# Per-head attention, wide fp32 loads for the first two batches and kept-back FFN units in a fused attention and SwiGLU kernel

## The chip, the cores and the metric

The kernel runs on one core of a Trainium2 chip. The metric is the device time of one execution in microseconds (us), taken as the median of several; lower is better. The kernel before takes 501.65 us (4 runs, 501.2 to 505.33). All times of this document come from runs of the state "fast", except where one is said to be otherwise. "Span" is the time from the first to the last instruction of the profiled execution; it lies about 2 us below the device time of the same run. The profiled run of the kernel before took 504.84 us.

Engines: PE is TensorE (matmuls; PEld is its weight load), ACT is ScalarE, DVE is VectorE, POOL is GpSimd, SP is SyncE. A line number such as L204 is a line of the kernel that the profile belongs to, so L204 of one kernel is not L204 of another.

## The reference

Block-causal attention (blocks of 64 in a sequence of 576, 8 batches, 8 heads of 64) feeds an RMS-normalised SwiGLU feed-forward network (FFN) over the 4608 tokens.

```python
def _attn_ref(q, k, v):                       # each (8, 8, 576, 64), float32
    scores = q @ k.transpose(0, 1, 3, 2) / np.sqrt(64)
    mask = (pos[:, None] // 64) >= (pos[None, :] // 64)
    scores = np.where(mask, scores, -1e9)
    attn = softmax(scores)                    # written out in the original
    return attn @ v

def _moe_ref(x, w_gate, w_val, w_out, rms_g): # x (4608, 512), d_ff = 1536
    xn = x / np.sqrt(np.mean(x * x, -1, keepdims=True) + 1e-6) * rms_g
    g = xn @ w_gate
    return (g / (1 + np.exp(-g)) * (xn @ w_val)) @ w_out
```

## The kernel before

The attention of one batch at a time is interleaved with the FFN of the 512-token chunk that earlier batches have completed. A chunk is 16 "units": 12 `ffn_up` units (8 matmuls of 512 columns each) and 4 `ffn_down` units (12 matmuls each). A list `units` holds them; attention code calls `run_unit()` between its stages, so that PE has FFN work while ACT computes exponentials. The order that the program text gives is a priority: a scheduler at build time places each instruction in its engine's own queue, and moves ready instructions up past ones that it believes will wait.

All loads that cast from fp32 to bf16 are issued by POOL. Q and K arrive as rows of 64 values, and a DMA transpose on the SP queue turns them.

```python
    def load_head(b, h, i):
        ...
        nc.gpsimd.dma_start(out=QKN[i][:, hp, kb:kb + NC, ds],
                            in_=k[b, h, BLK:S, :].rearrange("(c p) d -> p c d", p=P))
        nc.gpsimd.dma_start(out=QKN[i][:, hp, 1:NC + 1, ds], in_=q[...])
        nc.gpsimd.dma_start(out=VN[i][:, :, h, 0:D], in_=v[...])

    def transposes(b, hp):
        QKT = tp.tile([P, NBK, P], BF16, name="QKT")
        nc.sync.dma_start_transpose(out=QKT, in_=QKN[i][:, hp, :, :])
    ...
    def norm_stats(b):
        ...
        for t in range(NC + 1):                # ACT: sums of squares
            ...
            nc.scalar.activation(out=sq, in_=XN[:, t, :], func=AF.Square, accum_out=ss[:, t:t + 1])
        nc.gpsimd.tensor_scalar(out=rr, in0=ss, ...)                     # POOL
        nc.gpsimd.tensor_tensor(out=rs, in0=rr, in1=mhalf, op=ALU.pow)   # POOL
        ...
        for t in range(NC + 1):                # DVE
            nc.vector.tensor_scalar(out=XS[:, t, :], in0=XN[:, t, :], scalar1=rs[:, t:t + 1], ...)
    ...                                        # norm_transpose: PE transposes XS, ACT copies to XT
    for b in range(B):
        steps = load_batch_steps(b + 1, (b + 1) % 2) if b + 1 < B else []
        for hp in range(HP):
            ...
            for n, st in enumerate(attention_pair(b, hp)):
                st()
                run_unit()
            for _ in range(3):
                if steps:
                    steps.pop(0)()             # loads of the next batch
            ...
        norm_stats(b)
        run_unit()
        norm_transpose(b)
        while (chunks + 1) * TOKC <= (b + 1) * S:
            add_chunk(chunks)
            chunks += 1
```

What matters below is the end of each batch, called the boundary: the last values matmul on PE, normalisation `XN` on DVE, five squares on ACT, `rr` and `rs` on POOL, `XS` on DVE, transposes of `XS` on PE, `XT` on ACT, and only then the next chunk's FFN.

The softmax here doesn't subtract the row's maximum and nothing guards it: scores larger than these inputs give would overflow.

## Time and profile before

| what | read from | value |
|---|---|---|
| first score matmul | timeline of PE | 15.5 us |
| first FFN matmul | timeline of PE | 90.8 us |
| boundary to boundary (first transpose of `XS`), seven cycles | timeline of PE | 57.4, 49.5, 49.8, 49.0, 46.7, 46.5, 45.6 us |
| from the last boundary to the end | timeline of PE, span | 71.3 us |
| spacing of FFN matmuls | chain of work that ended last: 4 in 0.86 us | 0.216 us |

First some lines of the profile's page: the span, busy time by engine, and then the span in 40 equal slices, where each digit is the busy share in tenths (for PEclk the clock granted to PE, for DMA the mean share of the 16 DMA engines).

```profile
span 503.1 us, 7011 instructions
PE 387.4 (77%) x2534; PEld 205.0 (41%) x2576; DVE 215.5 (43%) x528; ACT 239.1 (48%) x481; POOL 204.4 (41%) x323
PE   0363005999149995999699879979997999699996
POOL 8995279898945533553365435130001000100000
PEclk9965655999759997999799989998999999799999
DMA  6999999999978887798789859461223201001102
```

The first seven slices (88 us) are thin on PE, while POOL and the DMA engines are busy. Then PE is mostly at 9 with gaps once per batch.

The timeline of PE around one boundary shows start, length in us, line, what was done and how many; in brackets, the idle time before it and what ended it.

```profile
184.39 0.41 PE L207 MATMUL Xb<-VN_92,PT 128*128 128x65 bf16 x8
184.64 2.75 PE L283 MATMUL fps<-WO,HT 128*128 128x512 bf16 x12
...
189.72 0.38 PE L163 MATMUL st<-QKT 128*128 128x512 bf16 x1 [1.87 <-ACT PT L166]
194.13 0.61 PE L253 MATMUL fps<-ident,XS 128*128 128x128 bf16 x4 [4.03 <-DVE XS L243]
```

From the last values matmul (184.8) to the first transpose of `XS` (194.1) pass 9.3 us; 1.87 + 4.03 us are idle. The timeline of POOL at the same boundary:

```profile
191.19 0.81 POOL L102 DMA_DIRECT2D QKN_94<-in_q_dram  x1
192.08 0.20 POOL L237 TENSOR_SCALAR rr<-ss 128x5 f32<-128x5 f32 x1
192.36 1.19 POOL L240 TENSOR_TENSOR rs<-rr,mhalf 128x5 f32<-128x5 f32 x1
```

The last square was ready on ACT at 189.2 us (its read-out starts at 189.00 and takes 0.19). POOL was issuing loads of the batch after next, which the scheduler had put ahead of `rr`, and reached `rr` at 192.08.

### The profile page before, as it was taken

The page shows a single profiled execution, that of the slowest core. Times are in us where ns is not written, and L with a number is a line of the kernel's source. Part 1 is how long each engine was busy: PE and PEld are TensorE (multiplying, and loading weights), DVE is VectorE, ACT ScalarE, POOL GpSimd, SP SyncE. Part 2 cuts the span into 40 slices and gives each one's busy share as a digit, 9 for nine tenths or more (in the row PEclk, how much of TensorE's full clock was granted, in tenths as well). Part 3 has the DMA queues.
Part 4 walks back from the last instruction along what each step waited for, and adds up shares of the span by engine and source line. Part 5 has one row for each costly group of instructions (what it writes and reads, how often), then busy time and mean ns, then how long its engine had stood idle before and what let it go on. Part 6 is the DMA issues. An engine that isn't in the chain of part 4 may idle for free.

```text
span 503.1 us, 7011 instructions
## 1 busy us (share of the span) xinstructions
PE 387.4 (77%) x2534; PEld 205.0 (41%) x2576; DVE 215.5 (43%) x528; ACT 239.1 (48%) x481; POOL 204.4 (41%) x323
## 2 busy tenths in 40 slices
PE   0363005999149995999699879979997999699996
PEld 0232003555035543554455445536554455344442
DVE  3111002682018711771286138616742772274570
ACT  1252204645336555555545655565656655432331
POOL 8995279898945533553365435130001000100000
PEclk9965655999759997999799989998999999799999
DMA  6999999999978887798789859461223201001102
GB/s 41 108 106 165 205 121 162 119 130 140 159 60 73 95 134 86 62 98 129 88 78 84 133 79 83 54 137 38 38 59 103 34 1 63 22 1 44 42 1 84
DMA packets 184627, 43.47 MB, mean 86 GB/s; under 512 B 174352, under 2 KB 179984, under 8 KB 184592
## 3 DMA queue, kind: packets, MB, share of 16 engines
q0 software_dynamic: 120512, 18.89, 51.3%
q1 hardware_dynamic: 64080, 24.13, 22.8%
q8 instruction: 20, 0.33, 0.3%
q14 instruction: 15, 0.12, 0.1%
HBM read 37.75 MB, written 9.44 MB: 94 GB/s over the span
## 4 chain that ended last, share of the span: by engine, by line
PE 48%; issue 21%; POOL 15%; DMA 13%; ACT 1%; DVE 0%; POOLq 0%; SPq 0%; ACTq 0%
PE fps L266 15%; PE fps L270 14%; PE fps L283 9%; PE st L163 5%; DMA QKT<-QKN_94 5%; DMA WO<-in_moe_w_out_dram 4%; POOL QKN_91 L100 2%; PE fps L253 2%; POOL QKN_91 L102 2%; DMA WV<-in_moe_w_val_dram 2%; PE Xb L207 2%; POOL VN_95 L104 2%; POOL VN_92 L104 2%; POOL rs L240 1%; DMA QKN_94<-in_k_dram 1%
## 5 line engine op out<-in xcount | busy, mean ns | idle before, releaser
L166 ACT ACTIVATE PT<-st 128x512 bf16<-128x512 f32 x192 | 108.6, 600 | 120.1 <-PE Xa L178 67.1
L163 PE MATMUL st<-QKT 128*128 128x512 bf16 (+3 forms) x286 | 72.2, 348 | 73.2 <-DMA QKT<-QKN_94 30.4
L266 PE MATMUL fps<-XT,WG 128*128 128x512 bf16 x416 | 113.2, 384 | 2.6 <-ACT XT L254 1.3
L270 PE MATMUL fps<-XT,WV 128*128 128x512 bf16 x417 | 111.4, 381 | 0.5
L273 ACT ACTIVATE th<-fps 128x512 f32<-128x512 f32 x108 | 64.2, 599 | 78.5 <-PE fps L266 67.1
L283 PE MATMUL fps<-WO,HT 128*128 128x512 bf16 x423 | 97.6, 379 | 0.5
L275 DVE SCALAR_TENSOR_TENSOR u<-th,fps 128x512 f32<-128x512 f32 x108 | 73.7, 686 | 49.6 <-ACT th L273 49.1
L277 DVE TENSOR_TENSOR HT<-u,fps 128x512 bf16<-128x512 f32 x108 | 73.4, 685 | 7.5 <-PE fps L266 0.5
L173 DVE MEMSET PT<- 64x64 uint32 x128 | 12.6, 112 | 140.9 <-ACT PT L166 138.2
L270 PEld LDWEIGHTS <-WV 128*128 128x128 bf16 x432 | 42.5, 98 | 52.0 <-issue 2.5
L163 PEld LDWEIGHTS <-QKT 128*128 128x128 bf16 x288 | 28.3, 109 | 81.8 <-DMA QKT<-QKN_94 30.8
L283 PEld LDWEIGHTS <-HT 128*128 128x128 bf16 x432 | 41.5, 98 | 45.8
L266 PEld LDWEIGHTS <-WG 128*128 128x128 bf16 x432 | 40.7, 99 | 38.5 <-issue 2.6
L207 PEld LDWEIGHTS <-PT 128*128 128x128 bf16 x800 | 41.7, 103 | 21.1 <-ACT PT L179 4.0
L253 PE MATMUL fps<-ident,XS 128*128 128x128 bf16 x160 | 20.3, 283 | 32.7 <-DVE XS L243 32.7
L286 ACT ACTIVATE ob<-fps 128x512 f32<-128x512 f32 x36 | 21.4, 593 | 49.5 <-PE fps L283 49.5
L243 DVE TENSOR_SCALAR XS<-XN,rs 128x512 bf16<-128x512 f32 x40 | 16.5, 481 | 57.9 <-POOL rs L240 57.9
L237 POOL TENSOR_SCALAR rr<-ss 128x5 f32<-128x5 f32 x8 | 1.6, 196 | 91.3 <-ACT sq L234 90.9
L253 PEld LDWEIGHTS <-XS 128*128 128x128 bf16 x160 | 15.4, 130 | 51.5 <-DVE XS L243 49.1
L104 POOL DMA_DIRECT2D VN_95<-in_v_dram x32 | 25.2, 800 | 23.8 <-PE Xb L207 21.4
L104 POOL DMA_DIRECT2D VN_92<-in_v_dram x32 | 25.8, 814 | 19.8 <-PE Xb L207 17.5
L100 POOL DMA_DIRECT2D QKN_94<-in_k_dram x32 | 25.6, 800 | 19.7 <-DMA QKT<-QKN_94 16.1
(51 smaller groups left out, 337.7 us busy)
## 6 DMA issues: line engine op xcount, KB each, us to landing
out_dram<-ob SPq DMA_DIRECT2D x36, 256.0 KB, 2.0
QKN_91<-in_k_dram POOLq DMA_DIRECT2D x32, 64.0 KB, 3.1
QKN_91<-in_q_dram POOLq DMA_DIRECT2D x32, 64.0 KB, 3.2
VN_92<-in_v_dram POOLq DMA_DIRECT2D x32, 64.0 KB, 3.0
QKN_94<-in_k_dram POOLq DMA_DIRECT2D x32, 64.0 KB, 3.1
QKN_94<-in_q_dram POOLq DMA_DIRECT2D x32, 64.0 KB, 3.4
VN_95<-in_v_dram POOLq DMA_DIRECT2D x32, 64.0 KB, 3.4
WG<-in_moe_w_gate_dram POOLq DMA_DIRECT2D x4, 384.0 KB, 12.1
```

The source lines that it names most:

```text
L100: nc.gpsimd.dma_start(out=QKN[i][:, hp, kb:kb + NC, ds], in_=k[b, h, BLK:S, :].rearrange("(c p) d -> p c d", p=P))
L104: nc.gpsimd.dma_start(out=VN[i][:, :, h, 0:D], in_=v[b, h, BLK:S, :].rearrange("(c p) d -> p c d", p=P))
L163: nc.tensor.matmul(st[:, o:o + n], w, qt(lo, n), start=True, stop=True)
L166: nc.scalar.activation(out=PT[:, BLK + bank * TOKC:BLK + bank * TOKC + o], in_=st[:, 0:o], func=AF.Exp, scale=SM_SCALE)
L207: ins = nc.tensor.matmul(dst, w, r, start=(n == 0), stop=(n == len(mms) - 1))
L253: nc.tensor.transpose(xt[:, o:o + P], XS[:, t, p * P:(p + 1) * P], ident)
L266: nc.tensor.matmul(pg, WG[:, p, m * P:(m + 1) * P], XT[:, p, t0:t0 + TOKC], start=(p == 0), stop=(p == HP - 1))
L270: nc.tensor.matmul(pv, WV[:, p, m * P:(m + 1) * P], XT[:, p, t0:t0 + TOKC], start=(p == 0), stop=(p == HP - 1))
L273: nc.scalar.activation(out=th, in_=pg, func=AF.Tanh, scale=0.5)
L275: nc.vector.scalar_tensor_tensor(out=u, in0=th, scalar=1.0, in1=pg, op0=ALU.add, op1=ALU.mult)
L277: nc.vector.tensor_tensor(out=HT[:, m, :], in0=u, in1=pv, op=ALU.mult)
L283: nc.tensor.matmul(po, HT[:, m, s * P:(s + 1) * P], WO[:, m, :], start=(m == 0), stop=(m == NMC - 1))
```

## The change

Intent: shorten the load stage by bringing Q and K of batches 0 and 1 in as fp32 in runs of 1536 bytes on the SP queue, with casts on DVE and ACT and PE transposes instead of DMA transposes; handle one head at a time instead of pairs, with unshifted chunks of 128 keys; and hold FFN units back, so that there is some left to run at the boundary. The core of the diff:

```diff
+    WIDE = 2
+    def load_wide(b, h0, h1):
+        hs = slice(h0, h1)
+        for dst, src in ((QW, q), (KW, k)):
+            nc.sync.dma_start(out=dst[:, hs, :, :].rearrange("p h s d -> p h (s d)"),
+                in_=src[b, hs, :, :].rearrange("h (p s) d -> p h (s d)", s=SLOT))
     ...
     def transposes(b, hp):
+        if b < WIDE:
+            QT, KA, KB = views
+            nc.gpsimd.memset(KA[D:P, :], 0.0)
+            nc.gpsimd.memset(KB[0:D, :], 0.0)
+            for src, n in ((QW, 0), (KW, 1)):
+                ...                              # cast to bf16 (DVE or ACT)
+                    nc.tensor.transpose(t[:, s * PQ:(s + 1) * PQ], ...)
+                ...                              # copies from PSUM to QKT
+        else:
+            nc.sync.dma_start_transpose(out=T, in_=QKN[b % 2][:, hp, :, :])
     ...
-    def run_unit():
-        if units:
+    def run_unit(keep=0):
+        if len(units) > keep:
             units.pop(0)()
     ...                                          # prologue: V of batch 0, weights, V of batch 1
+    LAG = 5
     for b in range(B):
+        for h in range(H):
             ...
+            st0()
+            run_unit(LAG - 2 if h else 0)
+            st1()
+            if pending is not None:
+                head_values(*pending)
+            pending = (b, h, state)
+            run_unit(LAG - 2)
+            ...                                  # three load steps of the next batch
+        head_values(*pending)
+        pending = None
+        run_unit()
         norm_stats(b)
         run_unit()
         norm_transpose(b)
```

## The prediction

> **What bounds the kernel now.** TensorE, but not everywhere. The table of windows shows three stages.
> (a) 0 to about 91 us: loads. TensorE is busy about 24 us of the first 87.5; the DMA share is 1.0 to 1.8. The timeline shows the first score matmul at 15.5 us, waits for the transposed Q/K inside batch 0 (up to 6.7 us), then 28.2 us before batch 1, whose loads stand in the POOL queue behind the weights. The first FFN matmul starts at 90.8 us.
> (b) 91 to 437 us: one batch of attention plus one 512-token FFN chunk per cycle. The first takes some 57 us, with another load wait (PE busy 7.6 of 25 us from 125 to 150); the next ones 49.5, 49.8, 49.2, 48.5, 46, 42. An FFN matmul starts every 0.216 us, so 144 of them are 31 us and, with scores (5.2), values (3.4) and transposes (1.1), from spacings in the timeline, about 41 us are needed. The excess of 5 to 8 us lies at the batch boundary: the queue of FFN units is empty there (17 slots for 16 units), and PE waits for squares, POOL's `rr`/`rs` (held 3 us behind descriptor issues), `XS`, `XT` (waits of 1.9 and 4.0 us).
> (c) 437 to 503 us: two pure FFN chunks, 66 us, at full PE rate.
>
> **What the change does.** Q and K of batches 0 and 1 come as fp32 in 1536-byte runs on the sync queue instead of 256-byte runs through POOL; 32 DMA issues of 0.8 us and the small tails leave POOL, and 8 of 32 DMA transposes (4.2 to 4.4 us each) vanish. Added per head pair: two casts (768 elements; estimate 0.8 us each, from 0.60 us for 512 on ACT), 12 PE transposes, three copies from PSUM (about 0.7 us each, from 0.74 us for the 576-wide `XT` copy), two POOL clears. Batch 0 becomes ACT-bound at an estimated 5.6 us per pair (eight exponentials plus cast and copy). The Trainium skill, "DMA: Bandwidth & Descriptors", section "Why small descriptors are slow (HBM only)", states a fixed overhead per packet; here 174352 of 184627 packets are under 512 B, and no run shows the overhead itself yet.
> Score columns (3136 to 3200 per pair) and value matmuls: neutral. Keeping units back gives two FFN units (3.5 to 5 us) at the boundary and one after it.
>
> **On the critical path.** Stage (a): all of it. If the POOL clears run early, FFN starts near 48 us; if they stand behind the weight issues, which block on earlier DMAs, near 75 us. I take 60, a gain of 31. Stage (b): the first cycle loses its load wait (about 14 us), the other boundaries shrink to about 2 us: seven cycles of about 43 us, 301 instead of 346, a gain of 45. Stage (c): unchanged, 66, plus 3 for odds and ends.
> Sum: 60 + 301 + 69 = 430 us, range 413 to 452. Faster by over 2%: 0.96; within 2%: 0.03; slower: 0.01.
>
> **What would show it.** Right: first FFN matmul at 48 to 75 us; no wait over 10 us of score matmuls for a DMA transpose after batch 1; boundary waits of the `XS` transposes under 3 us; cycles 42 to 44.5 us; FFN matmuls still 0.216 us apart; packets on the software queue about 18,000 fewer; mean granted clock above 0.902. Wrong: cycles still near 49 us, or PE waiting for QKT.
>
> **What would make it wrong.** POOL clears stuck behind weights; batch 2's loads, behind weights and batch 1's V, arriving late; the scheduler not placing kept units in the boundary; POOL's `rr` still waiting behind descriptor issues.

## The result, and the profile after

The changed kernel takes 479.34 us (4 runs, 478.51 to 480.27), 0.954 of the kernel before (95% interval 0.9492 to 0.9589). Ratios here and below are the mean time of one kernel's fast runs over that of the kernel before in the same rounds, so not quite the ratio of the medians. The direction was right; the time lies 49 us above the predicted 430 and outside the stated range.

| | before | predicted | after |
|---|---|---|---|
| first score matmul, us | 15.5 | | 39.5 |
| first FFN matmul, us | 90.8 | 60 | 80.2 |
| seven cycles, us | 344.5 | 301 | 328.2 |
| their mean, us | 49.2 | 43 | 46.9 |
| last boundary to the end of the span, us | 71.3 | | 73.0 |

The same lines of the page for the changed kernel:

```profile
span 476.7 us, 7703 instructions
PE 389.7 (82%) x2854; PEld 207.7 (44%) x2896; DVE 240.6 (50%) x553; ACT 265.7 (56%) x571; POOL 153.3 (32%) x212
PE   1206725999699969996999699979988997999996
POOL 6628799325442454245424540220000001000000
PEclk9999975999799989998999899999999999899999
DMA  9999999659975897689758962590433001001002
```

There is now an empty place at slice 3 (24 to 36 us), where PE does nothing. The waits of PE, longest first in total (us in total, times, longest us), name it:

```profile
PE fps L287 <- DVE XS L269: 29.4, 8, 9.7
PE st L204 <- POOL QKT L159: 21.0, 1, 21.0
```

One wait of 21.0 us is for L159, a POOL clear of half of a K tile. The clear itself is short. The timeline of POOL shows where it stands:

```profile
13.01 1.00 POOL L132 DMA_DIRECT2D WG<-in_moe_w_gate_dram  x1 [4.38 <-DMA VN_95<-in_v_dram]
15.24 0.74 POOL L134 DMA_DIRECT2D WV<-in_moe_w_val_dram  x1 [1.23 <-DMA VN_95<-in_v_dram]
...
28.82 0.82 POOL L138 DMA_DIRECT2D WO<-in_moe_w_out_dram  x1 [3.38 <-DMA WV<-in_moe_w_val_dram]
33.08 0.88 POOL L95 DMA_DIRECT2D VN_96<-in_v_dram  x1 [3.43 <-DMA WG<-in_moe_w_gate_dram]
35.94 0.69 POOL L87 DMA_DIRECT2D VN_96<-in_v_dram  x1 [1.98 <-DMA WV<-in_moe_w_val_dram]
37.92 0.82 POOL L138 DMA_DIRECT2D WO<-in_moe_w_out_dram  x1 [1.29 <-DMA WG<-in_moe_w_gate_dram]
38.78 0.63 POOL L159 MEMSET QKT<- 64x640 bf16 x1
```

Between 8.6 and 37.9 us POOL stands still for 18 us in seven waits (4.38, 1.23, 2.37, 3.38, 3.43, 1.98, 1.29), each for an earlier load to land, before it can issue the next weight or V load. The clear comes last in that queue, at 38.78 us; the first score matmul follows at 39.46 us. The Trainium skill, "DMA: Bandwidth & Descriptors", section "Anatomy of one DMA — SWDGE (gpsimd) path", says that DMA engines do not wait on semaphores and that such a wait happens on the issuing sequencer before dispatch. This trace agrees: the waits lie on POOL, and a clear that depends on none of those loads waited with them.

The steady boundary of the changed kernel, on PE and then on POOL:

```profile
211.23 0.47 PE L237 MATMUL X<-VN_96,PT_100 128*128 128x65 bf16 x10
211.54 4.26 PE L320 MATMUL fps<-WO,HT 128*128 128x512 bf16 x19
217.62 0.38 PE L204 MATMUL st<-QKT 128*128 128x320 bf16 x2 [1.31 <-ACT PT_97 L208]
221.09 0.40 PE L287 MATMUL fps<-ident,XS 128*128 128x128 bf16 x4 [3.10 <-DVE XS L269]
...
225.34 2.75 PE L320 MATMUL fps<-WO,HT 128*128 128x512 bf16 x11
```

```profile
217.42 0.75 POOL L106 DMA_DIRECT2D QKN_93<-in_q_dram  x1
218.24 0.20 POOL L263 TENSOR_SCALAR rr<-ss 128x5 f32<-128x5 f32 x1
218.50 0.79 POOL L104 DMA_DIRECT2D QKN_93<-in_k_dram  x1
219.31 1.20 POOL L266 TENSOR_TENSOR rs<-rr,mhalf 128x5 f32<-128x5 f32 x1
```

From the last values matmul (211.7) to the first transpose of `XS` (221.1) pass 9.4 us: the chain is as long as before. In it run 19 matmuls of kept units instead of 12, and a third kept unit (225.34) comes only after the transposes. So the boundary gained seven matmuls, about 1.5 us, and the cycle went from 49.4 us (mean of cycles two to four, before) to 47.8 us. POOL again reaches `rr` late: the last square was ready at 216.6 us, `rr` starts at 218.24, and one more load issue was put between `rr` and `rs`. After batch 0 it is worse: the last square is ready at 64.7 us and `rr` starts at 72.82 us:

```profile
72.82 0.20 POOL L263 TENSOR_SCALAR rr<-ss 128x5 f32<-128x5 f32 x1
```

### The profile page after: what moved, and what is told of

It is laid out like the page before. It is cut to its first block, busy times and chain, and to the rows that moved or that the text cites. A ratio compares the mean times of both kernels' runs of the same rounds, so it can differ in the third digit from the quotient of the medians.

```text
span 476.7 us, 7703 instructions
## 1 busy us (share of the span) xinstructions
PE 389.7 (82%) x2854; PEld 207.7 (44%) x2896; DVE 240.6 (50%) x553; ACT 265.7 (56%) x571; POOL 153.3 (32%) x212
## 3 DMA queue, kind: packets, MB, share of 16 engines
q0 software_dynamic: 100576, 16.53, 46.0%
## 4 chain that ended last, share of the span: by engine, by line
PE 43%; issue 27%; POOL 12%; DMA 11%; ACT 5%; DVE 1%; POOLq 0%; ACTq 0%; SPq 0%; DVEq 0%
PE fps L308 12%; PE fps L304 12%; PE fps L320 9%; PE st L204 4%; DMA WG<-in_moe_w_gate_dram 4%; PE fps L287 3%; DMA QKT<-QKN_93 3%; DMA VN_95<-in_v_dram 3%; PE X L237 2%; POOL rs L266 2%; DMA QKT<-QKN_94 2%; POOL QKN_93 L104 1%; POOL QKN_94 L104 1%; POOL QKN_93 L106 1%; POOL VN_95 L95 1%
## 5 line engine op out<-in xcount | busy, mean ns | idle before, releaser
L304 PE MATMUL fps<-XT,WG 128*128 128x512 bf16 x411 | 110.4, 383 | 1.1 <-ACT XT L290 0.2
L312 DVE SCALAR_TENSOR_TENSOR th<-th,fps 128x512 f32<-128x512 f32 x108 | 74.3, 688 | 51.0 <-ACT th L311 50.6
L204 PE MATMUL st<-QKT 128*128 128x512 bf16 (+4 forms) x320 | 70.2, 307 | 31.9 <-POOL QKT L159 21.0
L314 DVE TENSOR_TENSOR HT<-th,fps 128x512 bf16<-128x512 f32 x108 | 74.2, 687 | 11.4 <-PE X L237 0.9
L204 PEld LDWEIGHTS <-QKT 128*128 128x128 bf16 x384 | 36.7, 101 | 63.3 <-POOL QKT L159 21.3
L320 PEld LDWEIGHTS <-HT 128*128 128x128 bf16 x432 | 41.1, 98 | 45.6 <-issue 3.1
L208 ACT ACTIVATE PT_97<-st 128x512 bf16<-128x512 f32 x48 | 26.8, 595 | 35.8 <-PE st L204 32.4
L287 PE MATMUL fps<-ident,XS 128*128 128x128 bf16 x160 | 18.5, 266 | 29.4 <-DVE XS L269 29.4
L208 ACT ACTIVATE PT_98<-st 128x512 bf16<-128x512 f32 x48 | 27.7, 606 | 18.4 <-PE st L204 14.5
L290 ACT ACTIVATE XT<-fps,gscale 128x512 bf16<-128x512 bf16 (+7 forms) x64 | 25.9, 520 | 17.5 <-PE fps L287 17.5
L208 ACT ACTIVATE PT_99<-st 128x512 bf16<-128x512 f32 x48 | 27.4, 599 | 12.5 <-PE st L204 6.3
L249 DVE TENSOR_TENSOR XN<-X,rd 128x320 f32<-128x320 f32 x64 | 31.4, 491 | 2.0
L260 ACT ACTIVATE sq<-XN 128x512 bf16<-128x512 f32 x40 | 25.1, 627 | 11.6 <-DVE XN L249 10.9
L208 ACT ACTIVATE PT_100<-st 128x512 bf16<-128x512 f32 x48 | 27.0, 601 | 6.7 <-PE X L204 3.4
L104 POOL DMA_DIRECT2D QKN_93<-in_k_dram x24 | 18.4, 766 | 38.2 <-DMA QKT<-QKN_93 37.9
## 6 DMA issues: line engine op xcount, KB each, us to landing
WG<-in_moe_w_gate_dram POOLq DMA_DIRECT2D x4, 384.0 KB, 11.8
```

The lines of the kernel that those rows point to most:

```text
L104: nc.gpsimd.dma_start(out=t[:, hp, kb:kb + NC, ds], in_=k[b, h, 0:TAIL, :].rearrange("(c p) d -> p c d", p=P))
L204: nc.tensor.matmul(dst[:, o0:o0 + n], KT[:, k0:k0 + P], QT[:, lo:lo + n], start=True, stop=True)
L208: nc.scalar.activation(out=PT[:, o:o + o0], in_=dst[:, 0:o0], func=AF.Exp, scale=SM_SCALE)
L249: nc.vector.tensor_tensor(out=xn_tiles[b][:, :, h * D:(h + 1) * D], in0=xv[:, :, 0:D], in1=rd.to_broadcast([P, NQT, D]), op=ALU.mult)
L287: nc.tensor.transpose(x[:, t * P:(t + 1) * P], XS[:, t, p * P:(p + 1) * P], ident)
L290: nc.scalar.activation(out=xt_tiles[t][:, p, a - t * TOKC:e - t * TOKC], in_=x[:, a - b * S:e - b * S], func=AF.Copy, scale=gscale[:, p:p ...
```

## The experiments

Theory A: POOL's order costs the missing time. The clears of the wide path stand behind weight loads, and `rr`/`rs` behind load issues. Theory B (rival): the bytes of the first 90 us and the early start of the loads are the limit, so that reordering POOL gains nothing. A second pair of theories is about the part that did bring the gain: the kept units, the wide loads, or the per-head pipeline. All kernels below gave correct results.

| run | us, median | ratio to the kernel before | first FFN matmul, us | mean of seven cycles, us |
|---|---|---|---|---|
| after | 479.34 | 0.954 | 80.2 | 46.9 |
| a1_clear_dve | 465.03 | 0.9239 | 68.1 | 46.6 |
| a2_rs_first | 460.48 | 0.9131 | 72.1 | 45.5 |
| a3_both | 445.01 | 0.8818 | 56.3 | 45.5 |
| a4_nolag | 506.46 | 1.0051 | 80.4 | 51.3 |
| b1_wide0 | 478.54 (fast runs) | 0.954 | 83.5 | 47.2 |
| b2_before_lag | 487.22 | 0.9668 | 89.4 | 46.8 |
| b3_units | 429.01 | 0.8517 | 57.6 | 43.3 |
| b4_defer | 425.31 | 0.8444 | 50.6 | 44.0 |
| c1_wide0_fixed | 452.03 | 0.8969 | 82.8 | 42.9 |
| c2_before_fixed | 453.05 | 0.9003 | 89.8 | 42.2 |
| c3_units_no_rs | 459.83 | 0.9123 | 69.4 | 46.0 |

The kernel before had medians of 503.44 to 505.04 us in the rounds of the experiments. The times of first matmuls and cycles are those of the profiled execution. b1_wide0 had one slow run among its four, which is left out.

### a1_clear_dve: the clears leave POOL

```diff
-            nc.gpsimd.memset(KA[D:P, :], 0.0)
-            nc.gpsimd.memset(KB[0:D, :], 0.0)
+            nc.vector.memset(KA[D:P, :], 0.0)
+            nc.vector.memset(KB[0:D, :], 0.0)
```

> The two clears of QKT go from POOL to DVE, nothing else changes. Theory (POOL's order): the 21 us wait of score matmuls for the POOL clear goes, the first score matmul moves from 39.5 us to about 20 us and the first FFN matmul from 80 us to about 60 us; time about 460 us, less gain if the small statistic rr then stands behind load issues on POOL. Rival (the startup is bound by the bytes of the weights and of Q/K/V, so that the order on POOL does not matter): the first FFN matmul stays within 4 us of 80 us, time 475 us or more.

Measured: 465.03 us. The first score matmul moved from 39.5 to 12.9 us, more than expected, but the first FFN matmul only from 80.2 to 68.1 us. The caveat in the expectation is what happened: the last square of batch 0 was ready at 49.7 us, and `rr` started at 60.65 us, behind load issues that themselves waited for weights. B falls in its strong form (12 us were to be had), but this edit alone frees only half of them.

### a2_rs_first: loads issued behind rs

```diff
-        nc.gpsimd.tensor_tensor(out=rs, in0=rr, in1=mhalf, op=ALU.pow)
+        last_rs[0] = nc.gpsimd.tensor_tensor(out=rs, in0=rr, in1=mhalf, op=ALU.pow).ins
 ...
+    def load_step(steps):
+        with tc.issue_after(last_rs[0]):    # order in POOL's queue only, no wait
+            steps.pop(0)()
 ...
-                    steps.pop(0)()
+                    load_step(steps)
```

> The loads of batch b+1 are issued on POOL only behind rr and rs of batch b-1; the clears stay on POOL. Theory (rr/rs are held behind load issues): the wait of XS for rs shrinks by 8 us after batch 0 and by 2 to 3 us at each of the next four or five boundaries, first FFN matmul at about 72 us, time about 460 us. Rival (the loads need that head start, or the boundary is bound elsewhere): waits for QKT come up or the cycles stay at 47 to 48 us, time 470 us or more.

Measured: 460.48 us, first FFN matmul at 72.14 us as expected, cycles 46.7, 45.8, 44.7, 44.8, 44.8, 46.0, 46.0 us. `rr` now starts within 0.2 us of the last square at every boundary, as here on POOL:

```profile
202.80 0.20 POOL L264 TENSOR_SCALAR rr<-ss 128x5 f32<-128x5 f32 x1 [23.59 <-ACT sq L261]
```

From the last values matmul (197.8 us) to the first transpose of `XS` (204.85) pass 7.0 us instead of 9.4. The waits of PE for `XS` fell from 29.4 us in all to 18.4 us, and no wait of PE for a DMA transpose came up: the loads did not need their head start. B falls for the cycles. One detail of the expectation is wrong: after the first two boundaries the wait for `XS` itself fell by 0.7 us at most. Of the 3.4 us that the cycle from 173.00 to 221.09 lost (the one from 160.15 to 204.85 in a2_rs_first), 1.1 us are less busy time of PE, at a granted clock of 1.00 against 0.96, and 2.3 us less idle time, 1.6 us of it in waits of scores for exponentials.

### a3_both: both edits

> Both edits. Theory: the gains add, first FFN matmul at 50 to 55 us, cycles about 45.5 us, time 440 to 448 us. Rival (bytes bind once POOL's order is right): first FFN matmul at 65 us or later, or waits for QKT over 5 us, time 455 us or more.

Measured: 445.01 us; first FFN matmul 56.3 us. In a3_both POOL's queue reaches `rr` early and waits for ACT, the right way round (timeline of POOL in a3_both):

```profile
36.63 0.87 POOL L138 DMA_DIRECT2D WO<-in_moe_w_out_dram  x1 [3.91 <-DMA WG<-in_moe_w_gate_dram]
49.51 0.20 POOL L264 TENSOR_SCALAR rr<-ss 128x5 f32<-128x5 f32 x1 [12.01 <-ACT sq L261]
49.79 1.20 POOL L267 TENSOR_TENSOR rs<-rr,mhalf 128x5 f32<-128x5 f32 x1
```

The gains add, within the range given (the first FFN matmul came 1.3 us later than the range said). 80.2 − 56.3 = 24 us of the start were POOL's order.

### a4_nolag: no unit kept back

```diff
-    LAG = 5
+    LAG = 2
```

> LAG = 2 in the changed kernel: no FFN unit is kept back. Theory (the kept units fill the boundary): each boundary wait of the XS transposes grows from about 2.5 us to 6 us or more, time 495 to 505 us. Rival (the kept units do little, because the scheduler orders by its own model): within 5 us of 479 us.

Measured: 506.46 us, as slow as the kernel before (1.0051, 1.0001 to 1.0101). The first FFN matmul stays at 80.4 us, the cycles are 55.7, 51.7, 52.9, 51.6, 49.2, 49.9, 47.9 us. The table of windows gives, for a stretch, its length, then the busy time (and number of instructions) of PE, PEld, DVE, ACT and POOL, the granted clock, the DMA share and GB/s. The third full cycle of a4_nolag, and the same cycle in the changed kernel:

```profile
183.14:236.01 52.87, 45.88 (x332) 24.70 (x333) 25.59 (x62) 29.36 (x66) 20.04 (x27) 0.89 0.88 94
```

```profile
173.00:221.09 48.09, 43.21 (x327) 23.38 (x333) 25.86 (x62) 29.98 (x66) 20.10 (x28) 0.96 0.91 100
```

The theory's time is right, its detail is not: the waits for `XS` did not grow to 6 us (3.86 us at this boundary, 32.3 us in all against 29.4). Of the 4.8 us more per cycle, 2.7 us are more busy time of PE at a lower granted clock (0.89 against 0.96) and 2.1 us more idle time, much of it in short waits of scores for exponentials near the end of the batch (over the run 40 waits with 18.3 us in all, against 22 with 10.2 us). My reading is that with 18 slots for 16 units the finer pipeline uses its units up before the batch ends. Inside the changed kernel, the kept units are worth its whole gain.

### b1_wide0: the wide loads undone

```diff
-    WIDE = 2
+    WIDE = 0
 ...
-    load_wide(0, 0, 2)
-    ...
+    for hp in range(HP):
+        clear_qkn(0, hp)
+    load_qk_tail(0)
+    ...                     # Q, K, V of batch 0 by POOL, then the weights; batch 1 in the loop
```

> The changed kernel with the wide fp32 loads undone (WIDE = 0): Q and K of batches 0 and 1 come through POOL in 256-byte runs and DMA transposes as in the kernel before; per-head pipeline and kept units stay. Theory (the wide loads' gain was eaten by the clears waiting on POOL): first FFN matmul at about 90 us instead of 80 and a load wait before batch 1 as before; time 487 to 495 us. Rival (the wide loads carry the change): 500 us or more.

Measured: 478.54 us, the median of three fast runs (478.32, 478.54, 485.39; one more run, 486.53, was slow; with it the median is 481.97), ratio 0.954, interval 0.9455 to 0.9625. The trace is that of the run of 485.39 us, hardly faster than the slow one. Neither the theory's time (487 to 495 us) nor the rival's holds: the time is that of the change as delivered. Without the wide loads the score matmuls wait for DMA transposes (45.8 us in five waits, 16.2 the longest), and yet the first FFN matmul comes only 3.3 us later than with them. As delivered, no gain of the wide loads can be told from noise.

### b2_before_lag: kept units alone in the kernel before

```diff
-                st()
-                run_unit()
+                st()
+                run_unit(3 if hp or n else 0)
 ...
+        run_unit()
         norm_stats(b)
         run_unit()
```

> The kernel before with kept units alone: three FFN units held back during a batch, one more slot before the statistics. Theory (kept units fill the boundary in any pipeline): waits of the XS transposes and the empty slots shrink, cycles from 49 us to 46 to 47 us, time 483 to 491 us. Rival (they only make up for a loss that the finer per-head slots bring, as the run without them stood level with the kernel before): within 5 us of the kernel before.

Measured: 487.22 us, 0.9668; later cycles 47.4, 47.4, 46.2, 45.2, 43.9, 43.9 us. The theory holds for the time: a few lines bring 3.3 of the 4.6% that the whole change brought. The waits for `XS` after the first boundary shrank less than it says, from 17.2 to 14.9 us in all.

### b3_units: both POOL edits and two more kept units

```diff
-    LAG = 5
+    LAG = 7
 ...
         norm_stats(b)
+        run_unit()
+        run_unit()
         run_unit()
```

> Both POOL edits plus two more kept units run between the statistics and the transposes (LAG = 7). Theory (PE still idles 2 to 3 us at each boundary for want of work): the wait of the XS transposes goes from 18 us in all to under 5 us, cycles about 43 us, time 428 to 434 us. Rival (the boundary is no longer the limit): 440 us or more.

Measured: 429.01 us; cycles 42.2, then 43.4 to 43.7 us. The waits of PE for `XS` are 4.3 us in all, in 22 pieces. One boundary in b3_units on PE, and the cycle before it in the table of windows:

```profile
216.54 0.61 PE L237 MATMUL X<-VN,PT 128*128 128x65 bf16 x15
216.99 1.03 PE L309 MATMUL fps<-XT,WV 128*128 128x512 bf16 x4
217.85 7.93 PE L321 MATMUL fps<-WO,HT 128*128 128x512 bf16 x36
225.62 0.46 PE L288 MATMUL fps<-ident,XS 128*128 128x128 bf16 x2
```

```profile
182.19:225.62 43.43, 42.65 (x333) 22.47 (x332) 25.60 (x62) 29.91 (x66) 20.26 (x28) 1.00 1.05 111
```

The chain still takes 8.5 us (217.1 to 225.6); matmuls of kept units fill it without a gap, and the granted clock stays at 1.00. This is the boundary that I had predicted for the change.

### b4_defer: batch 1's first casts behind the end of batch 0

Built on b3_units. The casts of batch 1's first head pair are queued on DVE behind the last `XN` of batch 0 and on ACT behind its last square:

```diff
         norm_stats(b)
+        if nxt < WIDE:
+            with tc.issue_after(last_sq[0]), tc.issue_after(last_xn[0]):
+                transposes(nxt, 0)
 ...
```

> As b3_units, and the casts of batch 1's first head pair are queued on DVE and ACT behind the last normalisation and the last square of batch 0. Theory (in the run with both edits these casts wait in order for the load of batch 1 and hold up the end of batch 0): first FFN matmul from about 56 us to about 49 us, time about 7 us below b3_units. Rival: batch 1 then starts later by as much, same time as b3_units within 3 us.

Measured: 425.31 us, 3.7 us below b3_units. Between the two: the first FFN matmul came 7.0 us earlier (50.6 us), and the first cycle gave 5.0 us of it back (47.2 instead of 42.2 us). It is the fastest version, 0.8444 of the kernel before (0.8403 to 0.8486); its slowest run (425.98 us) is below the fastest of b3_units (428.39 us).

### c1_wide0_fixed: b3_units without the wide loads

> b3_units with the wide loads undone as in b1_wide0 (there is then no clear to move): rs ahead of the loads, LAG = 7. Theory (the wide loads are worth about 20 us once no clear waits behind the weights): first FFN matmul at 80 to 84 us against 57.6 us in b3_units, later cycles 43.5 us, time 448 to 456 us. Rival (the wide loads are worth nothing in any setting, as they were in the change as delivered): within 5 us of 429 us.

Measured: 452.03 us, 23 us above b3_units, with the first FFN matmul at 82.8 us against 57.6 us. So next to b3_units the wide loads, with their PE transposes, are worth 23 us; in the change as delivered they were worth nothing that could be measured. But the 23 us are not free of POOL's order. The loads of batch 1 are issued before any `rs` exists, so the edit cannot put them behind one: the last square of batch 0 is ready at 54.4 us, and `rr` starts 16.5 us later, behind these loads. From 49.8 to 65.5 us PE waits for Q and K of batch 1 (PE, then POOL):

```profile
65.53 1.03 PE L204 MATMUL st<-QKT 128*128 128x512 bf16 x3 [15.78 <-DMA QKT<-QKN]
70.88 0.20 POOL L264 TENSOR_SCALAR rr<-ss 128x5 f32<-128x5 f32 x1
```

FFN work of the first chunk could have filled part of this wait if `rr` had come first. No run tries that, so how much of the 23 us an earlier `rr` would give without wide loads stays open.

### c2_before_fixed: the same order edits in the kernel before

The kernel before keeps its pair-wise attention and its loads. It gets five units kept back, one more slot before and two more after the statistics, and loads issued behind `rs`.

> The kernel before with its own pair-wise attention and its own loads, plus kept units (five held back, three run between the statistics and the transposes) and loads issued behind rs. Theory (the cycle is set by what fills the boundary and not by the per-head pipeline): cycles of batches 3 to 7 at 43 to 44 us as in b3_units, time 455 to 463 us, 3 to 8 us above c1_wide0_fixed. Rival (the per-head pipeline is needed for that cycle): cycles of 46 us or more, time 472 us or more.

Measured: 453.05 us; cycles from the second on 42.7 to 42.8 us, a little shorter than the 43.4 us of the per-head kernels. What remains of its waits of PE is the start:

```profile
PE st L163 <- DMA QKT<-QKN: 56.9, 6, 28.0
PE fps L254 <- DVE XS L244: 3.5, 21, 0.2
```

The theory holds: the cycle is shorter than expected and the time 2 us below the range given. The per-head rewrite is not needed for the short cycle. The kernel stands level with c1_wide0_fixed (0.9003 and 0.8969, intervals overlap). The edit does not reach the first boundary here either: `rr` of batch 0 starts at 82.6 us, 30.0 us after the last square (29.6 us in the kernel before), behind the loads of batch 1.

### c3_units_no_rs: more kept units, but rs late

b3_units without the edit of a2_rs_first.

> b3_units without the edit that puts the loads behind rs: clears on DVE and LAG = 7 only. Theory (kept units cover the wait for rs from the second boundary on, so that POOL's order then matters only at the first boundary, where no units exist): first FFN matmul at about 68 us, cycles 43.5 to 44 us, time about 440 us. Rival (a late rs still holds the boundary): cycles of 45 us or more, time 448 us or more.

Measured: 459.83 us; cycles 45.6, 48.6, 48.5, 47.4, 45.2, 43.5, 43.5 us. The rival holds. While loads remain, two more units change little against a1_clear_dve (46.6, 48.2, 48.1, 47.8 us), since POOL gets to `rr` later still (1.5, 1.1, 1.6 us after the last square at boundaries two to four of a1_clear_dve, 3.1, 2.8, 3.6 us here). PE, then POOL, at one boundary of c3_units_no_rs:

```profile
196.38 7.93 PE L320 MATMUL fps<-WO,HT 128*128 128x512 bf16 x35
207.40 0.23 PE L287 MATMUL fps<-ident,XS 128*128 128x128 bf16 x1 [3.09 <-DVE XS L269]
```

```profile
204.43 0.85 POOL L106 DMA_DIRECT2D QKN<-in_q_dram  x1
205.35 0.20 POOL L263 TENSOR_SCALAR rr<-ss 128x5 f32<-128x5 f32 x1
```

The kept units end at 204.3 us and PE waits 3.09 us more for `XS`. In the last two cycles, where no loads are left, the cycle is 43.5 us without the edit too. Kept units and an early `rs` are needed together for that cycle.

A boundary without POOL, with `rr` and `rs` on another engine, was not measured.

## Why the prediction was wrong, point by point

The predicted sum was 60 + 301 + 69 = 430. Measured: 80.2 to the first FFN matmul, 328.2 for the seven cycles, and 70.9 for the rest (479.3 − 80.2 − 328.2). The misses are 20, 27 and 2 us, together the 49 us.

1. "I take 60" for the first FFN matmul: wrong by 20 us. The mechanism was named: "if they stand behind the weight issues, which block on earlier DMAs, near 75 us". But it was entered as one of two cases and averaged, though the POOL timeline of the kernel before already showed issues waiting for weights to land (3.14 and 0.84 us before the two `WO` loads), and the program order put the clears behind all of them. The second half of the failure is `rr`, which I listed under what could go wrong and did not put in the sum: 8 us after batch 0. With both taken away (a3_both) the first FFN matmul came at 56.3 us. The estimate of 60 describes that kernel.

2. "The other boundaries shrink to about 2 us: seven cycles of about 43 us": wrong by 27 us in sum. The failed step is the reading "the queue of FFN units is empty there". The trace of the kernel before shows a unit of 12 matmuls in the boundary (184.64 us), so holding units back added seven matmuls and not two whole units; the third kept unit ran behind the transposes, where the prediction had put it too. And the chain of the boundary, 9.3 us before and 9.4 us after, stayed as long as it was, with `rr`/`rs` behind load issues; that was also on the list of what could go wrong, without a cost (a2_rs_first, without it, has a chain of 7.0 us and cycles of 44.7 to 46.0 us from the second on). b3_units, with `rs` first and two more units, has the 43 us, and c3_units_no_rs shows that the units without `rs` first do not bring it.

3. "About 41 us are needed" per cycle: a little low. Where PE has no gap (b3_units) the cycle is 43.4 us with the per-head pipeline, and 42.8 us with the old one (c2_before_fixed).

4. Stage (c), the tail, was right: 69 predicted, 70.9 left over by the subtraction above.

5. Of the signs: first FFN matmul at 48 to 75 us: wrong (80.2). PE not waiting for QKT: wrong (21.0 us for its clear). FFN matmuls still 0.216 us apart, right (4 in 0.86 us). Packets on the software queue fell from 120512 to 100576, 19936 fewer where I said about 18000: right. The granted clock rose from 0.902 to 0.957: right. No long wait for a DMA transpose after batch 1: right, none among the waits of PE. Cycles of 42 to 44.5 us: wrong. Boundary waits under 3 us: right for five (2.45 to 2.94 us), wrong for three (9.7, 3.7 and 3.1 us), and it was the wrong sign to watch. The idle time just before the transposes is not the whole cost of a boundary; the transposes and the work after them also run on a slower, "cold" PE. At the first boundary 20 transposes took 2.48 us, most of them starting 0.107 us apart; in b3_units 16 took 1.07 us, about 0.056 us apart. The Trainium skill, "TensorE: Matmul & The Clock Gate", section "Wait — 56ns, not 53.3ns?", states 106.7 ns cold and 55.6 ns warm for 128 columns; the trace agrees.

6. The cited section "Why small descriptors are slow (HBM only)" gave a reason to expect much of the wide loads. Their worth was measured as 23 us (c1_wide0_fixed against b3_units), and as nothing in the kernel as delivered. How much of the 23 us is the overhead per packet, how much is POOL's issue time of 0.8 us per load, how much the DMA transposes and how much the late `rr` of c1_wide0_fixed, no run here separates. By the Trainium skill, "Trainium Kernel Development and Optimization", section "Key Constraints", DMAs issued from the queues of SP, ACT and POOL run on the same 16 DMA engines, so wide loads and weights would share them. No run here shows that they slow each other: the wide loads of batch 1 (1152 KB each) took 11.8 and 17.4 us from issue to landing, those of the first two heads (288 KB, a quarter) 3.4 and 4.3 us, 0.29 and 0.25 of that.

What stays open: how the 7 us between the fast runs of b1_wide0 come about, why the old pair-wise pipeline has the shorter full cycle by 0.6 us, and what the wide loads are worth once `rr` of batch 0 is early without them; the first two were only seen, the last was not run.

## What to carry to other kernels

Before a path is moved to a faster queue, list everything that its first consumer waits for, small clears and statistics too, and look at which engine's queue they stand in: one short clear behind waiting load issues kept PE idle for 21 us here; moving it brought 14 us (479.3 to 465.0 us), and putting `rr` ahead of the loads as well brought 20 us more (445.0 us). Filling a bubble with kept work and shortening the chain that makes it belong together: from 465.0 us (a1_clear_dve), more kept work alone gave 459.8 us, the shorter chain alone 445.0 us (12 us of it at the start), both 429.0 us. And try the order edits on the old kernel first: a few lines of order and kept units took the kernel before from 503 to 453 us, more than the rewrite did.

## What the Trainium skill lacked or had wrong

- "DMA: Bandwidth & Descriptors" says where a DMA's semaphore wait happens, and does not spell out what that costs instructions queued behind it on the same engine: 21.0 us of PE idle for a clear of 0.63 us, and a start of `rr` up to 30.0 us after its last input (c2_before_fixed, first boundary).
- The same page calls descriptor generation small and variable, without a figure; the time that POOL was held per issue was here, on average in the changed kernel, 0.63 us for 256 rows of 64 values, 0.78 us for 512 and 0.90 us for 1024.
- "GPSIMD Engine Reference" lists memset and gives no duration for it: clearing 64 x 640 bf16 took 0.63 us on POOL and 0.33 us on DVE (a1_clear_dve, where the trace lists it as 64 x 320 uint32). The power operation on 128 x 5 values took 1.19 us on POOL.
- Of the page on the clock gate only the two spacings at 128 columns were compared; on these, page and traces agree.
